# Moving remainders to VectorE, weight transfers to SP and weight rounding forward in a fused attention, expert and SwiGLU kernel

## The chip, the cores and the metric

One core of one Trainium2 chip. The metric is the time of one execution on the device in microseconds (us). The profile is that of one execution on the same core.

## What is computed

Three layers in float32. Masked attention over 4 x 8 heads of 576 positions; a soft mixture of 8 experts whose gates are balanced by 8 rounds of normalising rows and columns; a SwiGLU layer behind an RMS norm. The inputs of the last layer's weights come as 64-bit floats.

```python
# attention gives x: 2304 tokens x 512
P = np.exp(logits - logits.max())            # 2304 x 8, logits = x @ w_gate
for _ in range(8):
    P /= P.sum(1, keepdims=True) + 1e-09
    P /= P.sum(0, keepdims=True) + 1e-09
    P *= N / E
for e in range(E):                           # 8 experts, 512 -> 1024 -> 512
    out += P[:, e:e+1] * (np.maximum(x @ w1[e], 0.0) @ w2[e])
xn = x / rms * rms_g                         # then 512 -> 1536 -> 512
silu = g * (1.0 / (1.0 + np.exp(-g)))        # g = xn @ w_gate
return (silu * (xn @ w_val)) @ w_out
```

## The kernel before

**Two-part numbers.** Every operand of a large matrix product is held as a rounded part and a remainder (`hi`, `lo`), and each product is three matmuls. ScalarE rounds, and another engine subtracts: `high` (L1156) and `low` (L1159) do so for the hidden values, L915 and L918 for the first weights, L1033 and L1036 for the second weights.

**The order of the work.** Attention and expert 0 come first, with plain products. Experts 1 to 7 then run as 42 groups, (expert, half of the hidden width, third of the tokens); three groups in a row, one for each third, share their weights. A group has two rounds `r`, and a round has seven products of a seven-product (Strassen-like) scheme, in the order of the list `PROD`: each product is six matmuls of 384 columns into one of two banks `ub` (L1131). Behind each product, 12 slots later, comes one unit of the second layer, nine matmuls of 256 columns into the banks `db` (L1724), which `evict_1` adds into `acc` (L1748). The last layer runs as passes of the same kind.

**Between the layers.** `outcome_1` empties the bank of each product: three times a copy on ScalarE (L1270), three times a sum on VectorE (`with_more`, L1163), then the ReLU (L1278). `combos` makes four sums and differences of the blocks on GpSimd (L1238, L1243, L1250, L1257). Each of the seven combinations is split by `high` and `low`; the remainders of products 2, 5 and 6 are made on GpSimd (`LOW_POOL`), the other four on VectorE.

**Queues written out by hand.** `Background` counts slots (`now`), two for each product in the groups. A `Queue` holds steps with a lag each and runs a step when its lag has passed since the step before; one that `yields` also waits, in the last expert and the last layer, while an estimate of VectorE's backlog is more than `AHEAD` over that of TensorE (`matmuls`, `vector`, `room`), unless more than 8 steps wait. `prep` makes the first weights: `load_1` fetches the raw block of a region into `raw_1`, and `combine` makes from it the seven combinations and their two parts, in seven steps. There is one `raw_1`, and two regions in use, one for each round. `prepare_1` puts the whole region of the next three groups into the queue when the last round that uses it is over. `prep2` does the same for the second weights, product by product. `conv` turns the last layer's 64-bit weights into float32, 72 items from group 5 on (L830 to L854), through the buffer `cv` and DRAM tensors `m2d`. All these transfers are issued by GpSimd; the blocks of x (`load_block`, L1063) are issued by SP, which waits for the product that last uses the place.

**Toward the last layer.** In the last three groups each third of the tokens is scaled (`norm_scale`: ScalarE squares, GpSimd takes the root, L1369 multiplies), transposed on TensorE (`turn_tile`, L1379) at the slots of `TURN_AT`, and turned into the blocks of the next scheme (`norm_blocks`), which go to DRAM (`xnd`) and come back as x.

Of the kernel before, what the change touches and what calls it, by code (L numbers as in the profile page):

```python
# [17 lines left out]
P = 128  # L18
# [8 lines left out]
class Background:  # L27
# [53 lines left out]
class Queue:  # L81


    def __init__(self, clock, yields=False):
        self.clock = clock
        self.yields = yields
        self.items = []
        self.last = 0
        clock.queues.append(self)
# [23 lines left out]
def kernel(  # L113
# [95 lines left out]
    bg = Background()  # L209
    fin, prep, prep2, conv = Queue(bg), Queue(bg, True), Queue(bg), Queue(bg)  # L210

# [601 lines left out]
    def convert(nm, f, half):  # L813

        n = KC * P // 2
        raw = cv[:, : 2 * n].bitcast(U32)
        pair = raw.rearrange("p (n t) -> p n t", t=2)
        a, t = cv[:, 2 * n : 3 * n].bitcast(U32), cv[:, 3 * n : 4 * n]

        def load():  # L820
            if nm == "o":
                nc.gpsimd.dma_start(out=raw, in_=m2_out[f * P : (f + 1) * P, half * 2 * n : (half + 1) * 2 * n])
            else:
                src = (m2_gate if nm == "g" else m2_val)[half * n : (half + 1) * n, f * 2 * P : (f + 1) * 2 * P]
                nc.gpsimd.dma_start(
                    out=raw.rearrange("p (c n) -> p c n", c=KC // 2), in_=src.rearrange("(c p) n -> p c n", p=P)
                )

        def head():
            nc.vector.tensor_scalar(out=a, in0=pair[:, :, 1], scalar1=0x7FFFFFFF, scalar2=None, op0=ALU.bitwise_and)  # L830
            nc.vector.tensor_scalar(
                out=t, in0=a.bitcast(F32), scalar1=LOW_HEAD, scalar2=HIGH_HEAD, op0=ALU.max, op1=ALU.min
            )
            return 410

        def number():
            nc.vector.tensor_scalar(
                out=a, in0=t.bitcast(U32), scalar1=3, scalar2=0x3FFFFFFF,
                op0=ALU.logical_shift_left, op1=ALU.bitwise_and,
            )  # L840
            nc.vector.scalar_tensor_tensor(
                out=a, in0=pair[:, :, 1], scalar=0xC0000000, in1=a, op0=ALU.bitwise_and, op1=ALU.bitwise_or
            )
            return 540

        def tail():
            nc.vector.tensor_scalar(out=t.bitcast(U32), in0=a, scalar1=0xFF800000, scalar2=None, op0=ALU.bitwise_and)
            nc.vector.scalar_tensor_tensor(
                out=t, in0=pair[:, :, 0], scalar=2.0**-52, in1=t, op0=ALU.mult, op1=ALU.mult
            )  # L850
            return 540

        def whole():
            nc.vector.tensor_tensor(out=t, in0=a.bitcast(F32), in1=t, op=ALU.add)  # L854
            return n

        def store():
            nc.gpsimd.dma_start(out=m2d[nm][:, f, half * n : (half + 1) * n], in_=t)
# [49 lines left out]
    def combine(at, raw):  # L908
# [14 lines left out]
        def first():  # L923
            round_(raw[:, :512], 0, 2)
            sum_(s1, a21, a22, ALU.add)
            return 256

        def second():
            round_(a22, 2, 1)
            rest(raw[:, :512], 0, 2)  # L930
            return 512

        def third():
            sum_(a21, a11, a21, ALU.subtract)
            sum_(s2, s1, a11, ALU.subtract)
            return 662

        def fourth():
            round_(tmp, 3, 2)
            rest(a22, 2, 1)  # L940
            sum_(a12, a12, s2, ALU.subtract)
            return 662

        def fifth():
            round_(a21, 5, 1)
            rest(tmp, 3, 2)
            return 512

        def sixth():
            round_(a12, 6, 1)  # L950
            rest(a21, 5, 1)
            return 256

        def seventh():
            rest(a12, 6, 1)
            return 256

        return [(READ, first)] + [(STEP, f) for f in (second, third, fourth, fifth, sixth, seventh)]

    def load_1(g, j):  # L960

        if g < E:
            for h in range(2):
                c0 = (j + h * (NF // 2)) * P
                nc.gpsimd.dma_start(
                    out=raw_1[:, 512 * h : 512 * (h + 1)].rearrange("p (c n) -> p c n", c=KC),
                    in_=w1[g][:, c0 : c0 + P].rearrange("(c p) n -> p c n", p=P),
                )
        else:
            for h in range(2):  # L970
                f = (g - E) * NG + j // 2 + h * (NG // 2)
                conv.drain(f)
                nc.gpsimd.dma_start(out=raw_1[:, 512 * h : 512 * (h + 1)], in_=m2d["gv"[j % 2]][:, f, :])

    raw_1 = fa[:, :1024]

    def prepare_1(g, j):

        prep.add(combine(region(g, j), raw_1), ("w1", g, j))
        n = (g, j + 1) if j < 3 else (g + 1, 0)  # L980
        if n[0] < E + NPASS:
            prep.add([(WRITE, lambda: load_1(*n))])

    def w2_place(g, f):
        return (3, 5, 4, 6)[f]

    def prepare_2(g, f):
# [3 lines left out]
        def load():  # L991
            conv.drain((g - E) * NG + f)
            nc.gpsimd.dma_start(out=t, in_=m2d["o"][:, (g - E) * NG + f, :])

# [12 lines left out]
    def second_weights(g, hh):  # L1007
# [7 lines left out]
        def load(r):  # L1015
            f = 2 * hh + r
            for h in range(2):
                rows = w2[g][(f + h * (NF // 2)) * P : (f + h * (NF // 2) + 1) * P, :]
                nc.gpsimd.dma_start(out=raw[r][:, 512 * h : 512 * (h + 1)], in_=rows)

# [146 lines left out]

    LOW_POOL = (2, 5, 6)

# [269 lines left out]
    with tc.manual_schedule():  # L1439
# [400 lines left out]
        for n, (g, hh, qd) in enumerate(groups):  # L1840
# [36 lines left out]
            for r in range(2):  # L1877
# [7 lines left out]
                for i, (wk, xk, which, begins) in enumerate(PROD):  # L1885
# [12 lines left out]
                    if not again:  # L1898
# [77 lines left out]
        for n, (p, qd) in enumerate(passes):  # L1976
# [10 lines left out]
            for j in range(NG // 2):  # L1987
# [16 lines left out]
                for ci, s in enumerate((2 * j, 2 * j + 1)):  # L2004
# [5 lines left out]
                    for i, (wk, xk, which, begins) in enumerate(PROD):  # L2010
# [26 lines left out]
                    if n % NQD == NQD - 1 and p + 1 < NPASS:  # L2037
                        prepare_1(E + p + 1, s)
                if done is not None:
# [41 lines left out]
```

## Time and profile before

| | |
|---|---|
| time, 3 runs | 2283.39, 2291.61, 2292.65 us; median 2291.61 |
| the profiled execution | 2289.89 us, span 2287.1 us, mean granted clock 0.962 |
| TensorE busy | 2079.8 us, 91% |
| VectorE busy | 1797.0 us, 79% |
| ScalarE busy | 1035.7 us, 45% |
| GpSimd busy | 1050.5 us, 46% |

TensorE's busy time is that of its matmuls, which are pipelined and whose ends are modelled, and it contains time at the lower clock. An engine's busy share is a mean over the whole span, over stages with different limits.

### The profile page before, as it was taken

Reading aid. Unit: us, or ns where it says so; the run is one execution under the profiler, and the core shown is the slowest. Engines: PE = TensorE matmul, PEld = TensorE weight load, DVE = VectorE, ACT = ScalarE, POOL = GpSimd, SP = SyncE. Lnnn points to the kernel's source line nnn. Section 1 sums busy time; section 2 is a strip of 40 time slices with the busy share of each in tenths; the row PEclk is TensorE's granted clock in tenths of the full one; section 3 lists DMA queues with packets and bytes.
Section 4 is the critical chain, followed back from the end, with each engine's and each line's share of the span. In section 5 each row is a group of like instructions: output and inputs, shape, how many; then the busy total and the mean of one; then the engine's idle time right before and its main releaser. Section 6 shows DMA issues by size and latency. Waiting matters only on the chain. (4 is left out here: it accounts for less than half of the span.)

```text
span 2287.1 us, 37972 instructions
## 1 busy us (share of the span) xinstructions
PE 2079.8 (91%) x13611; PEld 1978.1 (86%) x13611; DVE 1797.0 (79%) x3513; ACT 1035.7 (45%) x2515; POOL 1050.5 (46%) x1203
## 2 busy tenths in 40 slices
PE   8999998898979898988989898989899679999999
PEld 7888878898979898888888797989899678999998
DVE  4667557789899998889897989899978785555754
ACT  7766234544444444444444444444445444443432
POOL 6433115776655665656565665655655530000000
PEclk9999998999999999999989998999999889999999
DMA  7787756173444444352616253444335656332151
GB/s 183 189 222 202 231 190 218 61 263 121 160 136 144 141 148 152 128 189 91 228 65 235 81 205 108 170 138 143 128 129 175 194 152 207 111 138 97 46 188 75
DMA packets 248123, 353.50 MB, mean 155 GB/s; under 512 B 77504, under 2 KB 157568, under 8 KB 247936
## 3 DMA queue, kind: packets, MB, share of 16 engines
q1 hardware_dynamic: 225792, 281.67, 37.3%
q0 software_dynamic: 22144, 69.42, 9.4%
q8 instruction: 107, 1.75, 0.3%
q14 instruction: 80, 0.66, 0.1%
HBM read 289.69 MB, written 61.34 MB: 153 GB/s over the span
## 5 line engine op out<-in xcount | busy, mean ns | idle before, releaser
L1131 PE MATMUL ub<-xt,w1t 128*128 128x384 f32 x2328 | 492.7, 349 | 58.0 <-DVE fa L1163 31.9
L1131 PEld LDWEIGHTS ub<-xt,w1t 128*128 128x128 f32 x2328 | 412.9, 197 | 71.5 <-DVE fa L1163 38.0
L1131 PE MATMUL ub<-xx,w1t 128*128 128x384 f32 x1956 | 407.0, 345 | 58.4 <-DVE fa L1163 45.8
L1748 DVE SCALAR_TENSOR_TENSOR acc<-db,prob,acc 128x256 f32<-128x256 f32 x840 | 384.6, 511 | 26.8 <-PE db L1724 25.9
L1724 PE MATMUL db<-w2t,ht 128*128 128x256 f32 x2772 | 393.8, 287 | 11.5 <-DVE ht L1159 9.9
L1131 PEld LDWEIGHTS ub<-xx,w1t 128*128 128x128 f32 x1956 | 340.8, 194 | 70.7 <-DVE fa L1163 50.6
L1724 PE MATMUL db<-w2t,hx 128*128 128x256 f32 x2520 | 365.5, 290 | 30.9 <-DVE hx L1159 29.5
L1724 PEld LDWEIGHTS db<-w2t,ht 128*128 128x128 f32 x2772 | 380.7, 195 | 14.9 <-DVE ht L1159 11.6
L1724 PEld LDWEIGHTS db<-w2t,hx 128*128 128x128 f32 x2520 | 349.5, 197 | 37.5 <-DVE hx L1159 33.0
L1278 ACT ACTIVATE fa<-fa 128x384 f32<-128x384 f32 x252 | 131.9, 524 | 469.2 <-DVE fa L1163 468.9
L1163 DVE TENSOR_TENSOR fa<-ub,fa 128x384 f32<-128x384 f32 x330 | 181.7, 552 | 187.8 <-PE ub L1131 174.2
L1156 ACT ACTIVATE ht<-fa 128x384 fp32r<-128x384 f32 x341 | 176.5, 520 | 110.7 <-POOL fa L1250 76.7
L1156 ACT ACTIVATE hx<-fa 128x384 fp32r<-128x384 f32 x313 | 161.9, 521 | 50.8 <-DVE fa L1330 35.2
L1270 ACT COPY fa<-ub 128x384 f32<-128x384 f32 x252 | 119.0, 473 | 141.5 <-PE ub L1131 136.0
L1159 POOL TENSOR_TENSOR ht<-fa,ht 128x384 fp32r<-128x384 f32 x140 | 150.6, 1079 | 49.9 <-ACT ht L1156 44.1
L1238 POOL TENSOR_TENSOR fa<-fa 128x384 f32<-128x384 f32 x84 | 91.7, 1091 | 173.2 <-ACT fa L1278 173.0
L1159 DVE TENSOR_TENSOR ht<-fa,ht 128x384 fp32r<-128x384 f32 x201 | 150.6, 751 | 16.4 <-ACT ht L1156 15.5
L1159 DVE TENSOR_TENSOR hx<-fa,hx 128x384 fp32r<-128x384 f32 x201 | 141.8, 705 | 21.8 <-ACT hx L1156 20.4
L1159 POOL TENSOR_TENSOR hx<-fa,hx 128x384 fp32r<-128x384 f32 x112 | 122.9, 1100 | 12.1 <-ACT hx L1156 9.3
L1036 DVE TENSOR_TENSOR w2t<-raw,w2t 128x256 fp32r<-128x256 f32 x168 | 106.8, 674 | 3.7 <-ACT w2t L1033 3.7
L918 DVE TENSOR_TENSOR w1t<-fa,w1t 128x256 fp32r<-128x256 f32 (+1 forms) x170 | 106.8, 636 | 1.2 <-ACT w1t L915 1.2
L1250 POOL TENSOR_TENSOR fa<-fa 128x384 f32<-128x384 f32 x84 | 87.7, 1044 | 40.2 <-DVE ht L1159 30.8
(285 smaller groups left out, 3653.5 us busy)
## 6 DMA issues: line engine op xcount, KB each, us to landing
xt<-xdt SPq DMA_DIRECT2D x111, 768.0 KB
xx<-xdt SPq DMA_DIRECT2D x92, 768.0 KB
xt<-xnd SPq DMA_DIRECT2D x25, 768.0 KB
xx<-xnd SPq DMA_DIRECT2D x24, 768.0 KB
fa<-in_moe_w_dram POOLq DMA_DIRECT2D x56, 256.0 KB, 4.1
raw<-in_moe_w_dram POOLq DMA_DIRECT2D x56, 256.0 KB, 5.7
xdt<-fa SPq DMA_DIRECT2D x14, 512.0 KB
xdt<-xt SPq DMA_DIRECT2D x54, 128.0 KB
```

The source lines that it names most:

```text
L918: nc.vector.tensor_tensor(out=at(7 + k, n), in0=src, in1=at(k, n).bitcast(F32), op=ALU.subtract)
L1036: nc.vector.tensor_tensor(out=w2_piece(k, r, 1), in0=(b21, b11, t4, t2, t1, t3, b22)[k][r], in1=w2_piece(k, r, 0).bitcast(F32), op=ALU.sub ...
L1131: nc.tensor.matmul(ps[:, :TH], w[i][:, c], x[:, k, c], start=first and c == 0 and n == 0, stop=c == 1 and n == 2, skip_group_check=True,)
L1156: nc.scalar.activation(h[0], src, func)
L1159: engine.tensor_tensor(out=h[1], in0=src, in1=h[0].bitcast(F32), op=ALU.subtract)
L1163: nc.vector.tensor_tensor(out=out, in0=ps, in1=more, op=ALU.add)
L1238: nc.gpsimd.tensor_tensor(out=z["S3"], in0=z["A11"], in1=z["A21"], op=ALU.subtract)
L1250: nc.gpsimd.tensor_tensor(out=z["S2"], in0=z["S1"], in1=z["A11"], op=ALU.subtract)
L1270: nc.scalar.copy(z[nm], ps)
L1278: nc.scalar.activation(z[nm], z[nm], AF.Relu)
L1724: nc.tensor.matmul(spot(k, m), hm[x], w[y], start=BEGIN[k] and r == 0 and m != 1 and i == 0, stop=r == 1 and i == 2, skip_group_check=True,)
L1748: nc.vector.scalar_tensor_tensor(out=a, in0=ps, scalar=prob[:, ti, g : g + 1], in1=a, op0=ALU.mult, op1=ALU.add)
```

## The change

Remainders of all seven products are made on VectorE. The first weights of the next three groups are made in five pieces while the last round still runs, each behind the last product that uses its blocks (`PARTS_AT`: piece by product), in eleven finer steps, 1.2 slots apart (`PACE`) and no longer 1.5. All transfers of weights and of the conversion are issued by SP. The conversion's next load stands behind its last sum, and its queue yields without a limit. The transposes of the third and second last group come two or three slots later. The estimates of the queues' clock get other constants.

```diff
     def matmuls(self, n, columns):
-        self.pe += n * (columns * 2 // 5 + 13)
+        self.pe += n * (columns * 5 // 12 + 14)
...
-            self.dve = max(self.dve, self.pe) + columns + 150
+            self.dve = max(self.dve, self.pe) + columns * 25 // 24 + 100
...
-        while self.items and self.last + self.items[0][1] < self.clock.now and (not self.yields or len(self.items) > 8 or self.clock.room()):
+        while self.items and self.last + self.items[0][1] < self.clock.now and (not self.yields or len(self.items) > self.limit or self.clock.room()):
...
-    TURN_AT = ((26, (0,)), (27, (1, 2)), (28, (3,)), (29, (4, 5)))
+    TURN_AT = ((28, (0,)), (29, (1, 2)), (31, (3,)), (32, (4, 5)))
...
+    PACE = 1.2
+    PARTS_AT = {0: 0, 1: 1, 3: 2, 5: 3, 6: 4}
...
-    fin, prep, prep2, conv = Queue(bg), Queue(bg, True), Queue(bg), Queue(bg)
+    fin, prep, prep2, conv = Queue(bg), Queue(bg, True), Queue(bg), Queue(bg, True, 10**9)
...
-                nc.gpsimd.dma_start(out=raw, in_=m2_out[f * P : (f + 1) * P, half * 2 * n : (half + 1) * 2 * n])
+                nc.sync.dma_start(out=raw, in_=m2_out[f * P : (f + 1) * P, half * 2 * n : (half + 1) * 2 * n])
...
-                conv.add([(0.5, convert(nm2, f2, half2)[0])], f)
-            conv.add([(STEP, whole), (WRITE, store)], f)
+                conv.add([(STEP, whole), (1, convert(nm2, f2, half2)[0]), (2, store)], f)
+            else:
+                conv.add([(STEP, whole), (WRITE, store)], f)
...
-        return [(READ, first)] + [(STEP, f) for f in (second, third, fourth, fifth, sixth, seventh)]
+        return (
+            [(READ, first)], [(PACE, second), (PACE, third), (PACE, fourth)], [(PACE, fifth), (PACE, sixth)],
+            [(PACE, seventh), (PACE, eighth), (PACE, ninth)], [(PACE, tenth), (PACE, last)],
+        )
...
-    def prepare_1(g, j):
-
-        prep.add(combine(region(g, j), raw_1), ("w1", g, j))
+    def prepare_1(g, j, part=None):
+
+        if part is None:
+            for part in range(5):
+                prepare_1(g, j, part)
+            return
+        if part == 0:
+            stages[g, j] = combine(region(g, j), raw_1)
+        prep.add(stages[g, j][part], ("w1", g, j))
         n = (g, j + 1) if j < 3 else (g + 1, 0)
-        if n[0] < E + NPASS:
+        if part == 4 and n[0] < E + NPASS:
             prep.add([(WRITE, lambda: load_1(*n))])
...
-    LOW_POOL = (2, 5, 6)
+    LOW_POOL = ()
...
+                    if ends and i in PARTS_AT:
+                        nxt = (groups[n + 1][0], 2 * groups[n + 1][1] + r) if n + 1 < NGP else (E, r)
+                        prepare_1(*nxt, PARTS_AT[i])
                     second(14 * n + 7 * r + i)
-                if ends:
-                    if n + 1 < NGP:
-                        prepare_1(groups[n + 1][0], 2 * groups[n + 1][1] + r)
-                    else:
-                        prepare_1(E, r)
```

The other four transfers (L825, L858, L965 and L973, L993, L1019) change from `nc.gpsimd` to `nc.sync` in the same way. In `combine` the work is cut so that `first` to `fourth` sum, round and subtract for blocks 0 and 1, `fifth` and `sixth` for blocks 3 and 4, `seventh` to `ninth` for blocks 5 and 6, `tenth` and `last` for block 2. The passes of the last layer call `prepare_1` with the same pieces.

## Rows read from the trace of the kernel before

**Rows 1.** The page, part 1: busy us (share of the span) and instructions.

```profile
PE 2079.8 (91%) x13611; PEld 1978.1 (86%) x13611; DVE 1797.0 (79%) x3513; ACT 1035.7 (45%) x2515; POOL 1050.5 (46%) x1203
```

**Rows 2.** Busy time by stretch, groups 6 to 35 (ten cycles of three).

```profile
536.50:1608.20 1071.70, 956.96 (x6304) 935.04 (x6304) 971.85 (x1841) 469.42 (x1082) 642.64 (x715) 0.95 0.43 148
```

**Rows 3.** The same for the six rounds of groups 18 to 20, columns as named.

```profile
core 0: us, PE busy (x) PEld busy (x) DVE busy (x) ACT busy (x) POOL busy (x), PEclk, DMA share, GB/s
962.70:988.80 26.10, 20.14 (x116) 19.12 (x115) 25.96 (x45) 10.89 (x29) 18.19 (x20) 0.87 0.24 73
988.80:1005.60 16.80, 14.66 (x89) 13.93 (x90) 15.16 (x32) 7.50 (x18) 8.43 (x10) 0.90 0.81 294
1005.60:1020.90 15.30, 15.30 (x111) 15.30 (x110) 12.28 (x29) 6.48 (x15) 9.05 (x11) 1.00 0.23 70
1020.90:1035.20 14.30, 14.30 (x104) 14.30 (x103) 11.50 (x24) 6.74 (x14) 7.87 (x11) 1.00 1.01 368
1035.20:1053.40 18.20, 17.58 (x124) 17.10 (x122) 18.06 (x30) 7.04 (x16) 12.34 (x14) 1.00 0.26 94
1053.40:1071.40 18.00, 15.36 (x94) 14.83 (x95) 15.36 (x32) 8.26 (x19) 7.99 (x11) 0.91 0.17 52
```

**Rows 4.** Waits in the ten cycles: us in total, times, longest us.

```profile
POOL cv L825 <- DVE cv L848: 110.2, 35, 9.9
...
PE ub L1131 <- DVE fa L1163: 62.2, 44, 4.8
...
ACT ht L1156 <- POOL fa L1250: 58.6, 22, 3.7
...
DVE ht L1159 <- ACT ht L1156: 9.7, 9, 2.8
...
DVE hx L1159 <- ACT hx L1156: 5.9, 11, 0.7
```

**Rows 5.** Line 918 (remainders of first weights) in three of the rounds.

```profile
962.70:988.80 26.10, 2.95 (x5) 0.87 0.24 73
...
1035.20:1053.40 18.20, 0.67 (x1) 1.00 0.26 94
1053.40:1071.40 18.00, 1.92 (x4) 0.91 0.17 52
```

**Rows 6.** Line 921 (sums of first weights) in the same rounds.

```profile
962.70:988.80 26.10, 4.25 (x4) 0.87 0.24 73
...
1035.20:1053.40 18.20, 0.52 (x2) 1.00 0.26 94
1053.40:1071.40 18.00, 2.62 (x3) 0.91 0.17 52
```

**Rows 7.** Timeline of VectorE: start us, us, instruction.

```profile
1651.34 0.55 DVE L1159 TENSOR_TENSOR hx<-fa,hx 128x384 fp32r<-128x384 f32 x1
1651.81 1.26 DVE L1748 SCALAR_TENSOR_TENSOR acc<-db,prob,acc 128x256 f32<-128x256 f32 x3
```

**Rows 8.** Line 1159 alone in the ten cycles: VectorE, then GpSimd.

```profile
536.50:1608.20 1071.70, 179.82 (x240) 192.93 (x180) 0.95 0.43 148
```

**Rows 9.** VectorE's groups by line and shape, same stretch: first and last of 17.

```profile
L1748 DVE SCALAR_TENSOR_TENSOR acc<-db,prob,acc 128x256 f32<-128x256 f32 x540 | 226.6, 473 | 7.8 <-PE db L1724 7.2
...
L1036 DVE TENSOR_TENSOR w2t<-fa,w2t 128x256 fp32r<-128x256 f32 x20 | 19.0, 989 | 0.0
```

**Rows 10.** Busy time by stretch, groups 36 and 37, columns as in rows 3.

```profile
1608.20:1651.50 43.30, 34.23 (x214) 32.92 (x213) 41.43 (x76) 18.82 (x46) 24.06 (x28) 0.88 0.44 146
1651.50:1679.60 28.10, 28.10 (x202) 28.10 (x202) 17.85 (x36) 13.10 (x29) 16.23 (x20) 1.00 0.65 217
```

**Rows 11.** The same for the conversion's buffer `cv` in group 36.

```profile
1608.20:1651.50 43.30, 0.00 (x0) 0.00 (x0) 11.34 (x17) 0.00 (x0) 2.51 (x5) 0.88 0.44 146
```

**Rows 12.** Waits of SP's queue, whole span: us, times, longest.

```profile
SPq L1063 <- PE ub L1131: 1517.3, 220, 81.8
```

**Rows 13.** TensorE's waits from 1760 to 1900 us.

```profile
PE db L1379 <- DVE acc L1369: 20.5, 6, 11.6
```

**Rows 14.** Timeline of TensorE in that stretch, with the idle time before.

```profile
1814.52 1.12 PE L1379 MATMUL db<-ident,acc 128*128 128x128 f32 x4 [11.62 <-DVE acc L1369]
```

More of the change, by code (lines that the diff above doesn't have):

```diff
@@ L81, with __init__ @@
 class Queue:
-    def __init__(self, clock, yields=False):
+    def __init__(self, clock, yields=False, limit=8):
         self.clock = clock
         self.yields = yields
+        self.limit = limit
         self.items = []
@@ L833, in head @@
             )
-            return 410
+            return n
         def number():
@@ L843, in number @@
             )
-            return 540
+            return 2 * n
         def tail():
@@ L850, in tail @@
             )
-            return 540
+            return 2 * n
         def whole():
@@ L857, in store @@
         def store():
-            nc.gpsimd.dma_start(out=m2d[nm][:, f, half * n : (half + 1) * n], in_=t)
+            nc.sync.dma_start(out=m2d[nm][:, f, half * n : (half + 1) * n], in_=t)
         return load, head, number, tail, whole, store
@@ L923, in first @@
         def first():
-            round_(raw[:, :512], 0, 2)
             sum_(s1, a21, a22, ALU.add)
@@ L928, in second, with third, fourth, fifth @@
         def second():
-            round_(a22, 2, 1)
+            round_(raw[:, :512], 0, 2)
+            sum_(s2, s1, a11, ALU.subtract)
+            return 256
+        def third():
             rest(raw[:, :512], 0, 2)
             return 512
-        def third():
+        def fourth():
             sum_(a21, a11, a21, ALU.subtract)
-            sum_(s2, s1, a11, ALU.subtract)
-            return 662
-        def fourth():
+            return 256
+        def fifth():
             round_(tmp, 3, 2)
-            rest(a22, 2, 1)
             sum_(a12, a12, s2, ALU.subtract)
-            return 662
-        def fifth():
-            round_(a21, 5, 1)
+            return 256
+        def sixth():
             rest(tmp, 3, 2)
             return 512
-        def sixth():
+        def seventh():
+            round_(a21, 5, 1)
             round_(a12, 6, 1)
+        def eighth():
             rest(a21, 5, 1)
             return 256
-        def seventh():
+        def ninth():
             rest(a12, 6, 1)
             return 256
-        return [(READ, first)] + [(STEP, f) for f in (second, third, fourth, fifth, sixth, seventh)]
+        def tenth():
+            round_(a22, 2, 1)
+        def last():
+            rest(a22, 2, 1)
+            return 256
+        return (
+            [(READ, first)], [(PACE, second), (PACE, third), (PACE, fourth)], [(PACE, fifth), (PACE, sixth)],
+            [(PACE, seventh), (PACE, eighth), (PACE, ninth)], [(PACE, tenth), (PACE, last)],
+        )
     def load_1(g, j):
@@ L964, in load_1 @@
                 c0 = (j + h * (NF // 2)) * P
-                nc.gpsimd.dma_start(
+                nc.sync.dma_start(
                     out=raw_1[:, 512 * h : 512 * (h + 1)].rearrange("p (c n) -> p c n", c=KC),
@@ L972, in load_1 @@
                 conv.drain(f)
-                nc.gpsimd.dma_start(out=raw_1[:, 512 * h : 512 * (h + 1)], in_=m2d["gv"[j % 2]][:, f, :])
+                nc.sync.dma_start(out=raw_1[:, 512 * h : 512 * (h + 1)], in_=m2d["gv"[j % 2]][:, f, :])
     raw_1 = fa[:, :1024]
-    def prepare_1(g, j):
-        prep.add(combine(region(g, j), raw_1), ("w1", g, j))
+    def prepare_1(g, j, part=None):
[6 more added lines that the diff above has]
+        prep.add(stages[g, j][part], ("w1", g, j))
         n = (g, j + 1) if j < 3 else (g + 1, 0)
-        if n[0] < E + NPASS:
+        if part == 4 and n[0] < E + NPASS:
             prep.add([(WRITE, lambda: load_1(*n))])
+    stages = {}
     def w2_place(g, f):
@@ L992, in load @@
             conv.drain((g - E) * NG + f)
-            nc.gpsimd.dma_start(out=t, in_=m2d["o"][:, (g - E) * NG + f, :])
+            nc.sync.dma_start(out=t, in_=m2d["o"][:, (g - E) * NG + f, :])
         def high():
@@ L1018, in load @@
                 rows = w2[g][(f + h * (NF // 2)) * P : (f + h * (NF // 2) + 1) * P, :]
-                nc.gpsimd.dma_start(out=raw[r][:, 512 * h : 512 * (h + 1)], in_=rows)
+                nc.sync.dma_start(out=raw[r][:, 512 * h : 512 * (h + 1)], in_=rows)
         def sub(out, a, b):
@@ L2036 @@
                             bg.pump()
-                    if n % NQD == NQD - 1 and p + 1 < NPASS:
-                        prepare_1(E + p + 1, s)
+                        if n % NQD == NQD - 1 and p + 1 < NPASS and i in PARTS_AT:
+                            prepare_1(E + p + 1, s, PARTS_AT[i])
                 if done is not None:
```

2 lines of the change are left out of this document (1 added, 1 removed).

## The prediction

> **What bounds the kernel now.** I read the page's busy shares first, then the table by stretches, then the waits. Over the whole span VectorE is busy 79% [rows 1], which hides two different halves. From 1938 us on, and before 330 us, TensorE runs almost without gaps; there no edit of this diff can give much. The middle is the expert part: 42 groups of 14 products and 14 second-layer units each. In ten full cycles of three groups (1071.7 us, 107.2 a cycle) VectorE is busy 971.9 us, 91%, and TensorE 957 us at a granted clock of 0.95 [rows 2]. The reader should then look at one cycle in its six rounds of about seven products [rows 3]: the third and fourth rounds last 15.3 and 14.3 us with TensorE busy throughout; that is TensorE's floor. The first lasts 26.1 us, with VectorE busy 25.96 of it and the granted clock down to 0.87; the fifth lasts 18.2 with VectorE busy 18.06. [...] What ends TensorE's waits says the same: first the sum that empties its bank (62.2 us), behind other work in VectorE's queue [rows 4].
>
> **The parts of the change.** I sum VectorE's work by round, since a round that TensorE bounds swallows up to 2 or 3 us more of it, and a round that VectorE bounds grows or shrinks by all of it. All terms are for the cycle of [rows 3].
>
> *First weights in pieces.* Now the 18 VectorE operations of two regions (9 each) fall in the rounds as nine in the first (2.95 + 4.25 = 7.2 us), three in the fifth (1.2) and seven in the sixth (4.5) [rows 5, 6]; one lies across an edge. Counted in slots of the queue (two per product): now region 0 begins at slot 15 of the third group and region 1 at slot 6 of the next. After, region 0 runs from slot 1 to 16. Region 1 cannot begin before its raw data is loaded (19) and waited for (26), and ends at 38, that is slot 10 of the next group. The first round of [rows 3] begins at slot 4, so four of region 1's operations stay in it and five go to the sixth round; eight of region 0 fall in the fifth, one in the fourth. Nineteen operations took 12.9 us, 0.68 each; I take 0.60, for a reason given below. First round 7.2 to 2.4: -4.8. Fifth 1.2 to 4.8: +3.6. Sixth 4.5 to 3.0: -1.5. Fourth +0.6. The work is only moved; the gain is that it leaves the fullest round.
>
> *Remainders on VectorE.* Eighteen a cycle come over from GpSimd, three a round. VectorE's own show the price: undisturbed 0.55 us in the record, 0.47 from start to start when they follow one another [rows 7], so +1.4 a round. [...] The start times say 0.47, and I go by them.
>
> *What GpSimd no longer does.* VectorE's mean remainder takes 0.75 us, 179.8 over 240 [rows 8], 0.2 more than undisturbed; the operation with a PSUM operand always takes 0.473, the weight remainder from SBUF 0.99 where it meets GpSimd's differences [rows 9]. Mean less the shortest of its shape, over all seventeen such groups between those two rows, makes 232 us in ten cycles, 23 a cycle: time in which VectorE stands behind a GpSimd instruction. Of GpSimd's 642.6 us there [rows 2] the remainders are 192.9 [rows 8], 30%, and they leave; its DMA issues leave too. The relief lies between 0 (if the sums that stay on GpSimd take over the meetings) and half of 23 (if issues hold VectorE as well); I take 30%, 7.0, which also makes the 0.68 above about 0.60. By round, as the stretching lies now: 2.6, 0.9, 0.6, 0.6, 1.4, 0.9.
>
> *The sum of a cycle.* VectorE's work per round becomes: first 26.0 + 1.4 - 4.8 - 2.6 = 20.0, so the round goes from 26.1 to 20.2 (-5.9). Second 15.2 + 1.4 - 0.9 = 15.7 of 16.8 (-0.3, less of the lower clock). Third 13.1 of 15.3 and fourth 12.9 of 14.3: nothing, TensorE bounds them; should their cover fail, each costs 1 to 2. Fifth 18.1 + 1.4 + 3.6 - 1.4 = 21.7: the new crowd, +3.6. Sixth 15.4 + 1.4 - 1.5 - 0.9 = 14.4 (-0.6). Together -3.2 a cycle, -32 over ten. The cycle into group 3 and that into group 39 have no conversion work: -3 each.
>
> *Conversion.* Its steps take 12.5 slots an item in the kernel before and 12 in the changed one, so 72 items end in group 35 instead of 36. Group 36 lasts 43.3 us with VectorE busy 41.4, its neighbour, which has none, 28.1 [rows 10]; the conversion in it is 11.3 [rows 11]. Together with its lighter first round it can fall no further than TensorE's floor: -14. The other groups take 4% more conversion: +5 over all, in the rounds where it counts.
>
> *Queues.* Weight loads and conversion transfers go to SP, which already stands waiting for TensorE before the blocks of x for 1517 us [rows 12]. A conversion load waits for VectorE 3 us on average, 9.9 at most [rows 4]; a block of x is asked for nine products (some 18 us) before its use and needs about 3, so the slack of 14 is more than one such wait. Cost 0; two of the longest waits in a row would cost 5 us once. On GpSimd the same waits stood before the sums, so they come earlier.
>
> *Later transposes.* They wait 20.5 us for the scaling in six places [rows 13], 11.6 at one [rows 14]. Moved two or three slots (4 to 6 us) they would wait less, but what follows group 39 is late in turn: the blocks of the first pass must be stored and read back, and their making is put off by the same slots. Between -15 and +8; I take -3.
>
> Sum: -32 - 6 - 14 + 5 - 3 = -50. The profiled execution took 2289.9 (its span of 2287.1 and 2.8 around it); 2289.9 - 50 = 2240. The median shown, 2291.6, lies 1.7 above, which is within the runs' own 9 us. Half a percent, 11 us, is what a measurement here can tell from no change.
>
> **Rivals.**
> [...]
> (b) *The crowd only moves.* The fifth round takes what the first gives, or the relief behind GpSimd does not come (7 a cycle, some 5.5 of it in rounds that VectorE bounds): about 2290. For it: total work of VectorE hardly changes, 97.2 + 8.5 - 7 a cycle. Against: region 1's operations do leave a round that is 99% full.
> (c) *Remainders hold the queue: slower.* Those of products 5 and 6 are made from sums that GpSimd makes, rounded by ScalarE; standing in VectorE's in-order queue they would hold everything behind them, the emptying of TensorE's banks first. Twelve a cycle; ScalarE's waits for such a sum are 58.6 us in 22 places, 2.7 each [rows 4]. The gain is gone when each of the twelve waits 0.4 us; at a quarter of 2.7 they cost 8 a cycle, +80: 2320. For it: GpSimd's sums can get slower beside a busier VectorE. [...] Against: remainders of the same kind that VectorE makes now wait only 9.7 + 5.9 us in 240 [rows 4], 0.07 each, and GpSimd's queue gets shorter.
>
> **How the numbers follow.** The forecast has 0.50, with a range of its own of 2222 to 2262 (the ends of the relief and of the transposes). (a) 0.13, (b) 0.20, (c) 0.17. The range goes from 2200, just under (a), to 2300, past (b); it leaves out (c). Faster by over 0.5% (under 2280): 0.50 + 0.13 + a third of (b) = 0.70. Same: the rest of (b), 0.13. Slower: 0.17.
>
> **What the profile after would show.** Right: the first round near 20 us, the fifth near 22, third and fourth unchanged; VectorE's remainder nearer 0.68 than 0.75 in the mean; group 36 near 29 us; no wait of TensorE for a block of x. Wrong: VectorE waiting for ScalarE before remainders by tens of us (rival c), other VectorE operations as stretched as now (b), TensorE waiting for a DMA after 1800 us, or a fifth round above 24 us.

## The result and the profile after

The changed kernel takes 2208.85 us (median of four executions; one of them, at a mean granted clock of 0.706, took 2610.39 us and is left out of the ratio), the kernel before beside it on the same chip 2292.08: a ratio of 0.9643, 95% interval 0.9614 to 0.9672, 82 us less. The profiled execution took 2208.8 us, with a span of 2207.0. That is faster, as forecast, but by 81 us on the profiled execution and not by 50.

Where it went, stretch by stretch, between the two profiled executions (groups counted from the first ReLU of each):

| stretch | before | after | difference | the prediction's terms |
|---|---|---|---|---|
| start to group 0 | 328.5 | 327.8 | -0.7 | 0 |
| groups 0 to 5 | 208.0 | 204.7 | -3.3 | -3 |
| groups 6 to 35, ten cycles | 1071.7 | 1003.3 | -68.4 | -32 + 5 |
| groups 36 to 40 | 171.1 | 151.5 | -19.6 | -14 - 3 |
| group 41 to the end | 507.8 | 519.7 | +11.9 | -3 |
| around the span | 2.8 | 1.8 | -1.0 | 0 |

So the gain that was not foreseen lies in the ten cycles, 41 us of it, and the tail went the other way. First the page's busy shares of the changed kernel (columns as in [rows 1]):

```profile
PE 2058.2 (93%) x13611; PEld 1965.4 (89%) x13611; DVE 1800.0 (82%) x3765; ACT 1032.7 (47%) x2515; POOL 644.4 (29%) x659
```

Then its ten cycles and group 36, the six rounds of groups 18 to 20, and group 41 to the end (columns as in [rows 3]):

```profile
532.50:1535.80 1003.30, 934.59 (x6301) 920.05 (x6301) 962.08 (x2040) 467.19 (x1081) 344.68 (x320) 0.97 0.47 160
1535.80:1565.80 30.00, 28.96 (x197) 28.11 (x198) 29.79 (x61) 17.95 (x45) 14.52 (x13) 1.00 0.56 202
...
934.30:955.40 21.10, 18.25 (x96) 18.05 (x97) 20.93 (x47) 10.31 (x27) 7.79 (x8) 0.76 0.46 155
955.40:971.40 16.00, 15.27 (x108) 15.07 (x108) 15.76 (x34) 7.88 (x19) 4.21 (x4) 1.00 0.65 231
971.40:985.10 13.70, 13.70 (x100) 13.70 (x99) 12.43 (x30) 6.32 (x15) 4.05 (x4) 1.00 0.52 166
985.10:1001.30 16.20, 16.04 (x113) 15.84 (x112) 14.22 (x28) 6.67 (x15) 5.05 (x5) 1.00 0.92 330
1001.30:1016.80 15.50, 15.46 (x110) 15.26 (x109) 15.40 (x38) 8.02 (x20) 4.76 (x4) 1.00 0.15 45
1016.80:1035.00 18.20, 15.97 (x113) 15.56 (x111) 17.71 (x33) 7.69 (x18) 8.42 (x9) 1.00 0.12 38
...
1687.30:2207.00 519.70, 475.56 (x2514) 441.16 (x2512) 328.69 (x644) 202.71 (x451) 34.65 (x38) 0.96 0.40 133
```

Against [rows 2] the reader should subtract twice. VectorE's busy time fell by only 9.8 us (971.9 to 962.1), although some 90 us of remainders came to it. Its idle time in the ten cycles, the length less the busy time, fell from 99.8 to 41.2 us. Most of the 68 us is therefore time in which VectorE stood still before. Against [rows 3], all rounds but the first now run at a granted clock of 1.00; the first fell from 0.87 to 0.76. The fifth round, which was to become the new crowd, went from 18.2 to 15.5 us. One cycle has some scatter in the kernel before; the means over its ten are 25.3, 17.1, 15.3, 14.6, 17.6 and 17.3 us, after 21.1, 15.8, 13.7, 16.2, 15.5 and 18.1. The changed kernel repeats itself: its cycles take 99.2 to 100.7 us, where those before took 103.8 to 109.5.

Waits in the ten cycles of the changed kernel (who waits, for whom, us, times, longest):

```profile
POOL fa L1263 <- ACT fa L1303: 526.4, 60, 11.4
...
PE ub L1156 <- DVE fa L1188: 55.5, 21, 3.6
...
PE db L1749 <- DVE hx L1184: 12.9, 15, 1.6
DVE fa L1188 <- PE ub L1156: 12.1, 30, 0.5
...
DVE hx L1184 <- ACT hx L1181: 5.2, 15, 0.3
...
ACT ht L1181 <- POOL fa L1268: 2.4, 5, 0.5
...
DVE ht L1184 <- ACT ht L1181: 1.7, 5, 0.3
```

GpSimd now stands ready 526 us for a value that ScalarE still has to make; before, its queue stood in transfers that waited for VectorE [rows 4]. ScalarE's waits for GpSimd's sums, 58.6 us in [rows 4], are gone (L1275 is that sum here); those for the sum before it are 4.8 us (L1268, one of the two lines is shown). VectorE's waits before remainders are 6.9 us together (15.6 before), with 420 remainders and not 240: none of the tens of us of rival (c).

VectorE's groups in the same stretch (us in total, mean ns):

```profile
L1773 DVE SCALAR_TENSOR_TENSOR acc<-db,prob,acc 128x256 f32<-128x256 f32 x540 | 226.8, 474 | 4.7 <-PE db L1749 4.7
L1184 DVE TENSOR_TENSOR ht<-fa,ht 128x384 fp32r<-128x384 f32 x220 | 143.1, 652 | 1.7 <-ACT ht L1181 1.7
...
L1061 DVE TENSOR_TENSOR w2t<-raw,w2t 128x256 fp32r<-128x256 f32 x120 | 44.8, 413 | 0.0
```

The sum with a PSUM operand (L1773) is as it was in [rows 9], 474 ns. The remainders of the second weights from `raw` took 701 ns in the mean before (79.6 us of busy time) and now take 413, close to the shortest record of this shape, 406; the remainders of the hidden values went from 0.75 us [rows 8] to 0.64. The line of the kernel before:

```profile
L1036 DVE TENSOR_TENSOR w2t<-raw,w2t 128x256 fp32r<-128x256 f32 x120 | 79.6, 701 | 0.0
```

### The profile page after: what moved, and what is told of

Same layout as the page of the kernel before. It is cut to its first block, busy times and chain, and to the rows that moved or that the text cites. A ratio compares the mean times of both kernels' runs of the same rounds, so it can differ in the third digit from the quotient of the medians.

```text
span 2207.0 us, 37570 instructions
## 1 busy us (share of the span) xinstructions
PE 2058.2 (93%) x13611; PEld 1965.4 (89%) x13611; DVE 1800.0 (82%) x3765; ACT 1032.7 (47%) x2515; POOL 644.4 (29%) x659
## 4 chain that ended last, share of the span: by engine, by line
PE 50%; DVE 37%; DMA 4%; issue 3%; ACT 3%; POOL 1%; SPq 1%; DVEq 0%; ACTq 0%; POOLq 0%
PE ub L1156 22%; PE db L1749 11%; DVE acc L1773 9%; DVE ht L1184 4%; DVE fa L1188 4%; DVE hx L1184 4%; DVE w1t L922 3%; PE db L728 2%; PE db L727 2%; DVE w2t L1061 2%; PE db L726 2%; DVE fa L925 2%; PE psh L726 1%; PE psh L727 1%; PE psh L728 1%
## 5 line engine op out<-in xcount | busy, mean ns | idle before, releaser
L1156 PE MATMUL ub<-xt,w1t 128*128 128x384 f32 x2328 | 480.6, 343 | 50.4 <-DVE fa L1188 36.0
L1156 PEld LDWEIGHTS ub<-xt,w1t 128*128 128x128 f32 x2328 | 403.5, 193 | 60.6 <-DVE fa L1188 41.0
L1773 DVE SCALAR_TENSOR_TENSOR acc<-db,prob,acc 128x256 f32<-128x256 f32 x840 | 384.9, 512 | 25.6 <-PE db L1749 25.1
L1749 PE MATMUL db<-w2t,hx 128*128 128x256 f32 x2520 | 359.1, 287 | 16.7 <-DVE hx L1184 16.4
L1749 PEld LDWEIGHTS db<-w2t,hx 128*128 128x128 f32 x2520 | 344.0, 193 | 21.8 <-DVE hx L1184 21.3
L1263 POOL TENSOR_TENSOR fa<-fa 128x384 f32<-128x384 f32 x84 | 92.5, 1101 | 736.3 <-ACT fa L1303 736.3
L1184 DVE TENSOR_TENSOR ht<-fa,ht 128x384 fp32r<-128x384 f32 x341 | 222.8, 656 | 6.8 <-ACT ht L1181 6.1
L1184 DVE TENSOR_TENSOR hx<-fa,hx 128x384 fp32r<-128x384 f32 x313 | 200.0, 639 | 19.8 <-ACT hx L1181 18.0
L1268 POOL TENSOR_TENSOR fa<-fa 128x384 f32<-128x384 f32 x84 | 113.4, 1350 | 22.4 <-ACT fa L1299 19.9
L922 DVE TENSOR_TENSOR w1t<-fa,w1t 128x256 fp32r<-128x256 f32 (+1 forms) x170 | 115.4, 681 | 5.3 <-ACT w1t L919 5.3
L1275 POOL TENSOR_TENSOR fa<-fa 128x384 f32<-128x384 f32 x84 | 87.6, 1042 | 56.2 <-DVE ht L1184 47.4
L1282 POOL TENSOR_TENSOR fa<-fa 128x384 f32<-128x384 f32 x84 | 92.3, 1098 | 6.4
L925 DVE TENSOR_TENSOR fa<-fa 128x256 f32<-128x256 f32 x160 | 93.5, 589 | 0.2
```

What stands on the lines that cost most here:

```text
L922: nc.vector.tensor_tensor(out=at(7 + k, n), in0=src, in1=at(k, n).bitcast(F32), op=ALU.subtract)
L925: nc.vector.tensor_tensor(out=out, in0=x, in1=y, op=op)
L1156: nc.tensor.matmul(ps[:, :TH], w[i][:, c], x[:, k, c], start=first and c == 0 and n == 0, stop=c == 1 and n == 2, skip_group_check=True,)
L1184: engine.tensor_tensor(out=h[1], in0=src, in1=h[0].bitcast(F32), op=ALU.subtract)
L1263: nc.gpsimd.tensor_tensor(out=z["S3"], in0=z["A11"], in1=z["A21"], op=ALU.subtract)
L1268: nc.gpsimd.tensor_tensor(out=z["S1"], in0=z["A21"], in1=z["A22"], op=ALU.add)
```

## The experiments

Twelve kernels were run, all compared with the kernel before on the same chip. "A" below is the changed kernel, "B" the kernel before. The three theories that their expectations name: **1**, the prediction's own (VectorE's work leaves the fullest round, and VectorE stands less behind GpSimd instructions; who issues a transfer is worth nothing); **2**, the conversion's 12 slots an item put its work at the same place of every cycle; **3**, GpSimd's queue held the sums and remainders in it back, and taking transfers and remainders out of it is the gain. For e9 and e10 the numbers 1 and 2 mean two versions of the last, as their texts say. Gains in us are 2290 times what the ratio differs from 1.

**e1: remainders of products 2, 5 and 6 back on GpSimd.** In A:

```diff
-    LOW_POOL = ()
+    LOW_POOL = (2, 5, 6)
```

> The changed kernel with the remainders of products 2, 5 and 6 back on GpSimd. Theory 1 (crowd: the gain comes from VectorE's fullest rounds, by moved weights and by fewer waits behind GpSimd): VectorE loses 18 operations a cycle (8.5 us) and gets some 8 us of waits behind GpSimd back, so 2205 to 2230 us. Theory 2 (phase: the gain comes from the conversion, 12 slots an item, 7 items in the 84 slots of a cycle, which now falls at the same places in each cycle): the lock stays, all ten cycles equally long, 2200 to 2220. If the remainders' leaving GpSimd was the larger part of the gain: 2250 or more.

Measured 2210.06 us, 0.9663 (0.9649 to 0.9678) against 0.9643 for A: some 5 us, with intervals that overlap. In A the remainders' place decides almost nothing. GpSimd is busy 523.0 us in the ten cycles instead of 344.7, VectorE 942.5 instead of 962.1, and the ten cycles take 1003.7 instead of 1003.3.

**e2: the first weights of a region queued whole, at the end of the round.** In A:

```diff
-                    if ends and i in PARTS_AT:
-                        nxt = (groups[n + 1][0], 2 * groups[n + 1][1] + r) if n + 1 < NGP else (E, r)
-                        prepare_1(*nxt, PARTS_AT[i])
                     second(14 * n + 7 * r + i)
+                if ends:
+                    prepare_1(*((groups[n + 1][0], 2 * groups[n + 1][1] + r) if n + 1 < NGP else (E, r)))
```

> The changed kernel, but a whole region is put into the queue when the last round that uses it is over, as before, still in the eleven finer steps. Theory 1: the first round of a cycle gets 4.8 us of VectorE's work back, the fifth loses 3.6 that it could bear: 2245 to 2265 us. Theory 2: cycles stay equally long and the kernel stays at 2205 to 2225.

Measured 2222.15 us, 0.9711 (0.9693 to 0.973): the pieces are worth about 15 us in A. The first round is 23.3 us in the mean instead of 21.1, the fifth 14.3 instead of 15.5. Theory 1 had 2245 or more; the time lies in the range of theory 2, which e5 refutes.

**e3: the seven transfers issued by GpSimd again.** In A, seven lines of this kind:

```diff
-                nc.sync.dma_start(
+                nc.gpsimd.dma_start(
```

> The changed kernel with the weight and conversion transfers issued by GpSimd again. Theory 1: the issues held VectorE for 1.5 us a cycle, so +15 at most: 2209 to 2225 us. Theory 2: the lock stays: 2205 to 2215. Third possibility, that GpSimd's queue standing in waits before its sums was what made the cycles long and uneven: 2235 or more, with VectorE idle again for 8 us a cycle and more.

Measured 2245.39 us, 0.9814 (0.9797 to 0.983): 39 us, the largest part of the change as seen from its end. In the ten cycles (1029.0 us) GpSimd's queue stands again before the conversion's loads, and TensorE's wait for the sum on VectorE is 71.3 us where A has 55.5. The time is that of the third possibility, its sign is not: VectorE's idle time is 5.3 us a cycle where 8 and more was expected (A has 4.1), and its busy time rose by 13.5 us in the ten cycles.

```profile
PE ub L1156 <- DVE fa L1188: 71.3, 38, 3.6
POOL cv L828 <- DVE cv L851: 67.1, 30, 7.9
...
POOL cv L825 <- DVE cv L851: 46.8, 17, 8.4
```

**e4: the old places of the transposes.** In A:

```diff
-    TURN_AT = ((28, (0,)), (29, (1, 2)), (31, (3,)), (32, (4, 5)))
+    TURN_AT = ((26, (0,)), (27, (1, 2)), (28, (3,)), (29, (4, 5)))
```

> The changed kernel with the transposes at their old slots. The stretch from group 41 to the end is 12 us longer in the changed kernel, and TensorE stands 10.2 us there before the first block of x read back from DRAM. If the later transposes cause this, 2196 to 2202 us and that wait is gone; if the wait comes from the other parts (a first pass that is reached earlier), 2207 to 2215.

Measured 2204.32 us, 0.9636 (0.962 to 0.9652), by times no different from A. The profiles say more. From group 36 to the end of the span A takes 671.2 us and e4 664.2. TensorE's waits from 1640 to 1830 us, first A, then e4:

```profile
PE db L1404 <- DVE acc L1394: 10.6, 4, 4.0
PE ub L1156 <- DMA xt<-xnd: 10.2, 1, 10.2
```

```profile
PE db L1404 <- DVE acc L1394: 20.1, 6, 12.3
```

The later transposes wait 10 us less for the scaling, and TensorE then stands 10.2 us once, at 1724.5 us, before the first pass, for the block that they deliver late. That wait is gone in e4, though the time lies between the two ranges expected. It was in the prediction as a bound, not as the value taken.

**e5: the conversion at 12.5 slots an item.** In A:

```diff
-                conv.add([(STEP, whole), (1, convert(nm2, f2, half2)[0]), (2, store)], f)
+                conv.add([(STEP, whole), (1, convert(nm2, f2, half2)[0]), (2.5, store)], f)
```

> The changed kernel with the conversion's store half a slot later, so that an item takes 12.5 slots again and its steps drift through the cycle of 84 slots. Theory 2 (phase: 7 items in a cycle lock the schedule): cycles become uneven and the kernel loses 20 to 40 us: 2229 to 2249. Theory 1: only group 36 gets its conversion back, some 5 to 10 us: 2212 to 2220.

Measured 2206.19 us, 0.9644 (0.9628 to 0.966): no change. Theory 2 falls for A, and theory 1's 2212 to 2220 was missed as well. The ten cycles got 4.9 us shorter (998.4) and group 36, which now carries conversion again, 2.1 longer (32.1).

**e6: the remainders alone.** In B: `LOW_POOL = ()`.

> The kernel before with one edit: all remainders on VectorE. By the prediction's terms (+1.4 a round of VectorE, -7 a cycle of waits behind GpSimd's remainders) and by the run with this edit undone, which lay within 0.2% of the changed kernel: 2280 to 2300 us. Rival c of the prediction (remainders hold VectorE's queue for ScalarE): 2310 or more.

Measured 2251.67 us, 0.9842 (0.9828 to 0.9857): 36 us faster, more than any theory gave. Its ten cycles, and two of the waits in them:

```profile
532.50:1564.80 1032.30, 934.91 (x6309) 917.55 (x6307) 970.88 (x2022) 471.39 (x1081) 475.03 (x537) 0.97 0.44 154
```

```profile
DVE fa L1163 <- PE ub L1131: 15.8, 29, 1.4
...
ACT ht L1156 <- POOL fa L1250: 10.2, 9, 1.9
```

VectorE is busy as long as in [rows 2], 970.9 against 971.9 us, with 180 operations more: what they cost, it no longer loses behind GpSimd. The 39 us that the ten cycles lost are all idle time of VectorE (99.8 to 61.4). ScalarE waits 10.2 us for GpSimd's sums and not 58.6; VectorE's wait for TensorE's products falls to 15.8 us from 50.8 in B:

```profile
DVE fa L1163 <- PE ub L1131: 50.8, 42, 4.3
```

Rival (c) is refuted by the part alone.

**e7: the conversion's 12 slots alone.** In B:

```diff
-            conv.add([(STEP, whole), (WRITE, store)], f)
+            conv.add([(STEP, whole), (WRITE - 0.5, store)], f)
```

> The kernel before with one edit: the conversion's store half a slot earlier, so 12 slots an item. The prediction's term (group 36 free of conversion, the others 4% more): -9, so 2275 to 2285 us. Theory 2 (phase): -20 to -40, 2250 to 2270, and all cycles of one length.

Measured 2298.0 us, 1.0043 (1.0028 to 1.0058): slower by 10 us, against both expectations. Group 36 did fall from 43.3 to 34.0 us, but the ten cycles rose by 15.7 to 1087.4. Here the next load still stands before the last sum, so this is not the whole of what A does to the conversion.

**e8: the transfers by SP alone.** In B, the seven lines from `nc.gpsimd` to `nc.sync`.

> The kernel before with one edit: the seven transfers of weights and of the conversion issued by SP. The prediction's 0 for it: 2285 to 2295 us. Theory 3 (GpSimd's queue stands in the waits and issues of these transfers, and its sums come late for ScalarE and VectorE), after the run in which this edit was undone lay 1.7% over the changed kernel: 2250 to 2265, with VectorE's idle time in ten cycles falling from 100 us toward 50.

Measured 2241.36 us, 0.9793 (0.9776 to 0.981): 47 us faster, where the prediction had 0. Its ten cycles, and one group of VectorE in them:

```profile
532.10:1567.40 1035.30, 940.35 (x6311) 923.20 (x6310) 936.02 (x1842) 470.25 (x1080) 528.32 (x502) 0.96 0.44 153
```

```profile
L854 DVE TENSOR_TENSOR cv<-cv 128x256 f32<-128x256 f32 x67 | 39.2, 585 | 0.1
```

Here it is VectorE's busy time that falls, by 35.8 us, with the same operations; its idle time stays (99.3), where theory 3 expected it to fall toward 50 (and the time no lower than 2250). ScalarE's wait for the late sum shrinks, VectorE's wait for products hardly does:

```profile
DVE fa L1163 <- PE ub L1131: 47.8, 38, 4.2
...
ACT ht L1156 <- POOL fa L1250: 25.2, 10, 3.4
```

The conversion's last sum (L854) took 914 ns in the mean in B and takes 585: 22 us. In B:

```profile
L854 DVE TENSOR_TENSOR cv<-cv 128x256 f32<-128x256 f32 x67 | 61.3, 914 | 0.1
L848 DVE SCALAR_TENSOR_TENSOR cv<-cv 128x256 f32<-128x256 uint32 x67 | 33.0, 493 | 2.3
```

and in e8:

```profile
L848 DVE SCALAR_TENSOR_TENSOR cv<-cv 128x256 f32<-128x256 uint32 x67 | 41.8, 624 | 2.3
```

In B the next load waits in GpSimd's queue for the step just before that sum (L848); when it is let go, remainders or sums that stood behind it come next, and in some 28 of the 67 cases L854 runs beside one of them. Of the time by which L854 exceeded its shortest in B (some 34 us in 67), GpSimd's remainders stood over some 17 and its sums over some 13. But other steps got longer in turn, as L848 shows: the conversion's seven steps fell together from 263 to 254 us only.

A sum over all of VectorE's operations says more. In the ten cycles of B they took 249 us more than the shortest records of their shapes. Shared out by which record of GpSimd lay beside each, 112 us of this are GpSimd's sums, 75 its remainders, 30 the differences of the second weights (L1022) and 27 its DMA issues. In e8 it is 213 us: 105, 73, 29 and 0. Most of the 36 us is thus the issues' own time on GpSimd, beside which VectorE's operations were stretched. The sharing is an estimate from the overlap of the records.

**e9 and e10: which transfers.** In B, e9 moves only the conversion's three lines to SP, e10 only the four of the weight loads.

> The kernel before with only the conversion's transfers (load from 64 bits, store to DRAM) issued by SP; the weight loads stay with GpSimd. In the ten cycles of the kernel before these are 134 issues of 83 us in GpSimd's records, in front of which its queue stands some 228 us, most of it waiting for VectorE's next conversion step; the weight loads are 80 issues of 52 us with some 8 us of waits. All seven lines together gave -47. Theory 1, the waits in GpSimd's in-order queue held the sums behind them: nearly all comes from here, -38 to -47, 2243 to 2252. Theory 2, each issue costs by its own time, on GpSimd or by holding VectorE: in proportion 83 to 52, -29, about 2261. The prediction (queues cost nothing): 2285 to 2295.

> The kernel before with only the weight loads issued by SP; the conversion's transfers stay with GpSimd. Theory 1 (waits in the queue): 0 to -8, 2282 to 2290. Theory 2 (issue time): -18, about 2271. The prediction: 2285 to 2295.

Measured: e9 2264.54 us, 0.9911 (0.9881 to 0.994), -20 us; e10 2258.59 us, 0.988 (0.9847 to 0.9914), -27 us. Together they make e8's 47. The version by waits falls: the weight loads, in front of which GpSimd stood for 1 us (the 8 in the expectation count the waits before L1022, which is no transfer), gave no less than the conversion, with some 228. The version by issue time gave -29 and -18; it has the signs and the sum, and misses each half, e9 by a little over the interval's end (-27), e10 by a little under (-20). The profiles say that the halves work differently. VectorE's group of the conversion's last sum, in e9 and then e10:

```profile
L854 DVE TENSOR_TENSOR cv<-cv 128x256 f32<-128x256 f32 x67 | 44.4, 663 | 0.1
```

```profile
L854 DVE TENSOR_TENSOR cv<-cv 128x256 f32<-128x256 f32 x67 | 66.1, 986 | 0.1
```

and ScalarE's wait for a sum of GpSimd, in the same order:

```profile
ACT ht L1156 <- POOL fa L1250: 40.8, 14, 3.6
```

```profile
ACT ht L1156 <- POOL fa L1250: 31.5, 16, 3.4
```

In e9 VectorE's busy time falls by 19.2 us in the ten cycles and its idle time by 4.5; in e10 the idle time by 16.4 and the busy time by 5.9. By the sharing of e8, 15 us still lie beside the weight loads' issues in e9 and 12 beside the conversion's in e10.

**e11: remainders and issues both as before, the rest of the change kept.** A with the edits of e1 and e3.

> The changed kernel with both of the other two large parts undone: remainders of products 2, 5 and 6 on GpSimd, all transfers issued by GpSimd. What is left are the first weights in pieces, the conversion's 12 slots, the estimates and the later transposes. By the prediction's own terms (first round -4.8, fifth +3.6, sixth -1.5 in a cycle, group 36 -14): -30, about 2258. By the differences of the runs so far (the pieces gave 6 beside the remainders and 14 beside both; the 12 slots alone cost 10): 2275 to 2290.

Measured 2271.24 us, 0.9928 (0.9899 to 0.9957): -16 us, between the two expectations. Its first and fifth rounds in groups 18 to 20:

```profile
957.60:981.70 24.10, 18.10 (x102) 17.16 (x103) 23.93 (x44) 10.29 (x26) 16.57 (x19) 0.86 0.27 86
...
1026.10:1045.90 19.80, 17.35 (x111) 16.95 (x110) 19.33 (x35) 8.16 (x19) 14.56 (x15) 0.91 0.25 89
```

Here the forecast crowd does appear: the fifth round is 19.4 us in the mean of ten cycles, 1.8 over B, full of VectorE work, and the granted clock falls in it. It goes away once GpSimd is relieved of both: with its remainders or its issues left in place the fifth round is 16.9 us in the mean (e1) and 17.6 (e3), in A 15.5.

**e12: e4 and e5 together.**

> The changed kernel with the old TURN_AT and the conversion at 12.5 slots an item, the two edits that alone came out at 2204 and 2206. If the early transposes' -4 is real and the two are independent: 2200 to 2205, under the changed kernel by 0.2 to 0.4%. If both were scatter: 2207 to 2210.

Measured 2198.42 us, 0.9617 (0.9591 to 0.9643), 6 us under A; the intervals overlap, from 0.9614 to 0.9643. Its profile has both halves as e4 and e5 had them alone: ten cycles 998.4 us, from group 36 to the end of the span 664.6. It beats B clearly; that it beats A is supported by the profiles rather than settled by the times.

## Why the prediction was right in sign and short in size

The sign is right. The size is not: 2209 lies outside the forecast's own 2222 to 2262. It lies inside 2200 to 2300 because the lower end was drawn just under (a), 2207 us: the second and sixth rounds at the full granted clock, an estimate of 33 us in ten cycles from the 0.90 and 0.91 of [rows 3]. No run shows these 33 us, nor what lowers the clock; what the runs showed in their place is 1.00 in both rounds of groups 18 to 20 in A and at most 13 us by it, as told below. That 2209 lies inside the range is luck.

By round, in means of the ten cycles, A's lengths differ from B's by -4.2, -1.3, -1.6, +1.6, -2.1 and +0.8 us, where the sum had -5.9, -0.3, 0, 0, +3.6 and -0.6. The fifth round is the largest miss. Of the signs that the prediction named, the first round (21.1 us), the remainder (0.64), group 36 (30.0) and the blocks of x in the ten cycles came; the fifth round near 22 did not, and TensorE did wait for a DMA before the first pass, which stood under "wrong".

All kernels with the lengths of their ten cycles, in which the bulk lies (us; idle is the length less the busy time):

| kernel | ratio | ten cycles | VectorE busy | VectorE idle | GpSimd busy |
|---|---|---|---|---|---|
| B | 1 | 1071.7 | 971.9 | 99.8 | 642.6 |
| e7, 12 slots alone | 1.0043 | 1087.4 | 974.7 | 112.7 | 644.5 |
| e11, pieces and the rest | 0.9928 | 1043.8 | 975.1 | 68.7 | 650.6 |
| e9, conversion by SP | 0.9911 | 1047.9 | 952.6 | 95.3 | 579.0 |
| e10, weights by SP | 0.988 | 1049.4 | 966.0 | 83.4 | 595.9 |
| e6, remainders alone | 0.9842 | 1032.3 | 970.9 | 61.4 | 475.0 |
| e8, all by SP | 0.9793 | 1035.3 | 936.0 | 99.3 | 528.3 |
| e3, A with GpSimd issuing | 0.9814 | 1029.0 | 975.6 | 53.4 | 466.9 |
| e2, A with whole regions | 0.9711 | 1014.1 | 954.8 | 59.3 | 349.3 |
| e1, A with GpSimd's remainders | 0.9663 | 1003.7 | 942.5 | 61.2 | 523.0 |
| A | 0.9643 | 1003.3 | 962.1 | 41.2 | 344.7 |
| e4, A with early transposes | 0.9636 | 1003.3 | 961.9 | 41.4 | 344.5 |
| e5, A with 12.5 slots | 0.9644 | 998.4 | 947.0 | 51.4 | 351.1 |
| e12, e4 and e5 | 0.9617 | 998.4 | 945.6 | 52.8 | 352.6 |

*What bounds the kernel.* Right. The rounds that VectorE fills are those that moved, and A's first round is still filled by it (20.93 of 21.1 us).

*Queues at 0, and the issues left out of the relief: this is the step that failed.* The prediction compared SP's slack with the transfers' waits and found no cost, which held: SP now stands 413 us for VectorE before conversion loads, yet TensorE waits for no block of x in the ten cycles. (A block, put at about 3 us, had its 768 KB moved 3.7 to 4.3 us after its issue in the ten cycles of B, where none was under way before it.) But it gave no value to what GpSimd gains ("On GpSimd the same waits stood before the sums, so they come earlier"), and of the relief it took the remainders' share alone; that issues hold VectorE as well it named for the upper end only. The move was worth 47 us alone and 39 with the rest in place. In the ten cycles of e8 that is VectorE's shorter operations, 27 of 36 us beside the issues by the estimate above, and not its idle time. That the sums come earlier shows in ScalarE's wait for them, 25.2 us and not 58.6; that this is worth time by itself is not shown. SP's waits in A, whole span:

```profile
SPq L1088 <- PE ub L1156: 324.1, 150, 35.7
SPq L828 <- DVE cv L851: 282.6, 41, 10.2
...
SPq L825 <- DVE cv L851: 130.2, 20, 10.1
```

A single issue is small beside its transfer: that of a conversion load (L825) took 0.73 us on GpSimd in B, against a median of 3.2 from issue to landing. Summed they are not small here: 52 us of issues for the weight loads and 83 for the conversion left GpSimd in the ten cycles, and the time fell by some 27 and some 20.

*Remainders: +1.4 a round and -7.0 a cycle of relief.* The cost was right: remainders grew from 18.0 to 27.0 us a cycle, +9.0 against +8.4. The relief was under-sized: VectorE's time over the shortest of each shape fell from 25 us a cycle to 16 (the prediction had 23 for the first; the records sum to 249 in ten cycles, not 232), and its busy time from 97.2 to 96.2 where the sum had 98.7. The weight remainders of 0.99 us [rows 9] lay mostly beside issues of weight loads (L965, 27 records) and remainders on GpSimd (8), and beside none of its differences. The larger omission is idle time. The sum by rounds kept VectorE's waits as they stood and took only its work off; but VectorE waited 50.8 us for products, and ScalarE 58.6 for GpSimd's late sums. With GpSimd's remainders gone (e6) these fell to 15.8 and 10.2. With the transfers gone (e8) ScalarE's wait fell as well, VectorE's stayed at 47.8; and in e11, where GpSimd has as much to do as in B, VectorE's idle time fell by 31 us all the same. So that late sums of GpSimd stood behind VectorE's waits is argued for the remainders and not shown for the issues.

*The two overlap.* Remainders and issues both take GpSimd's time. Alone in B they give 36 and 47 us. With the rest of the change in place, e11, e3, e1 and A make a square: from e11, remainders on VectorE give 26 (e3), issues by SP 61 (e1), both 65 (A). Taken out of A they cost some 5 and 39: with the issues gone and the weights in pieces, another 178 us on GpSimd (e1) cost next to nothing.

*First weights in pieces.* Direction right, sizes off. Work of `combine` on VectorE went by -3.6 us in the first round (-4.8 predicted), +2.5 in the fifth (+3.6), +0.1 in the sixth (-1.5) and +1.2 in the fourth (+0.6). The fifth round's +3.6 in length did not come: in e11 it rose 1.8, in A it fell 2.1, because the relief behind GpSimd was larger there than the -1.4 taken: VectorE's time over the shortest is 4.6 us in this round in B, 5.7 in e11 and 1.4 in A. A's pieces are worth 15 us (e2).

*Conversion.* Group 36 came out at 30.0 (29 forecast). The +5 for 4% more work in the other groups was mis-sized: alone it cost 15.7 us in the ten cycles (e7), more than group 36 gave back. Beside the other parts it costs 4.9 (1003.3 against e5's 998.4). Why it is so dear in B, with VectorE's idle time up by 12.9, was not settled.

*Later transposes.* -3 was taken between -15 and +8; the profiles of A and e4 give +7 for the tail, the stored block being late as the upper bound had it.

*Rivals.* (b) is refuted by A's fifth round, (c) by e6 and by A's waits. That GpSimd's sums get slower beside a busier VectorE held for one of the four: L1268 took 1363 ns in the mean in A, and the same sum 1074 in B (L1243); the other three took 1030 to 1098 in A and 1035 to 1112 in B. (a), 2207 us, has A's time, and half of what it took: the second and sixth rounds no longer run at 0.90 and 0.91 but at 1.00. The second is 1.3 us shorter for it at most, 13 in ten cycles; the sixth is no shorter, since VectorE now fills 17.71 of its 18.2 us, and the first runs at 0.76 where it had 0.87. The time is thus not (a)'s, even though the number nearly is.

What stays open: how GpSimd's records and VectorE's fall against one another differs from kernel to kernel, and the issues' share of e8's 47 us was estimated from overlaps. A kernel in which GpSimd only waits and issues nothing was not tried. With the issuing engine the kind of queue changed too: in the ten cycles of B 47.33 MB went through the one that the profile calls software_dynamic, in e8 nothing did; the two changes cannot be told apart here. The new constants of the estimates, the yielding of the conversion's queue and the place of its load were not undone alone.

## What to carry to other kernels

Before a transfer's issue is called free, count what it takes on the issuing engine, and look at whose instructions run beside it: GpSimd was 60% busy and bounded no round, and taking 135 us of issues off it shortened VectorE's work by 36 (e8). When a sum of work by rounds is made, the waits of the bounding engine belong in it as a term, with the question which edit ends them. Gains of two edits that relieve the same engine did not add up here: they were 26 and 61 us one by one and 65 together, and the smaller was worth some 5 beside the other.

## What the runs showed of the hardware

The remainder of the second weights, L1061 on VectorE with two SBUF operands, ran at 413 ns in the mean in the changed kernel (shortest record 406), and at 701 ns in the kernel before (L1036); 180 operations moved from GpSimd to VectorE left VectorE's busy time unchanged (971.9 and 970.9 us, B and e6). The same operation on the same shape, L854, took 986, 914, 663 and 585 ns in the mean in e10, B, e9 and e8, which differ only in who issues the transfers, while the sum with a PSUM operand kept to 472 to 475 ns in all of these kernels. In the ten cycles of B a remainder of the hidden values on VectorE (L1159, two SBUF operands) took 548 ns in the mean where no record of GpSimd lay beside it (95 records, none over 554) and 884 where one did (145, up to 2086); in A (L1184) 548 (309) and 914 (111). The sum with a PSUM operand took 474 and 473 in B, without and with. A longer TensorE share at the lower clock in one round (0.76 and not 0.87) went with a faster kernel, in which every other round of the cycle was granted 1.00.
